# Attention with decaying state and a 16-item feed-forward: another written-out order, fewer VectorE operations for the powers of w, the count for the general path late, the output in 2 KB rows

## The chip, the cores and the metric

The kernel runs on one core of one Trainium2 chip. Its time is the device time of that core in microseconds (us); the profile's span runs from the first to the last instruction of one execution. The engines are called PE (TensorE, matrix products; PEld is its weight load), DVE (VectorE), ACT (ScalarE), POOL (GpSimd) and SP (SyncE, which here issues all transfers).

## What is computed

Four sequences, eight heads, 768 steps, head size 48. A state of 48 x 48 per sequence and head decays by `w` and takes up `k` and `v`; its product with `r` is the attention output. All heads of one step together (384 numbers) then pass a feed-forward of width 2048.

```python
for t in range(S):
    kt, vt, rt = k[:, :, t], v[:, :, t], r[:, :, t]
    cur = np.einsum('bhd,bhe->bhde', u[None] * kt, vt)
    y[:, :, t] = np.einsum('bhd,bhde->bhe', rt, state + cur)
    state = w[None, :, :, None] * state + np.einsum('bhd,bhe->bhde', kt, vt)
...
x = np.ascontiguousarray(attn_out.transpose(0, 2, 1, 3)).reshape(B * S, H * D)
h = x @ w_in
sp = np.maximum(h, 0.0) + np.log1p(np.exp(-np.abs(h)))
g = h * erf(sp)
return (g @ w_out).astype(np.float32)
```

## The kernel before

**Chunks.** The 768 steps are cut into six stretches of 128. One stretch of one sequence is a chunk; there are 24, numbered stretch by stretch, and four chunks of one stretch make a block of 512 tokens (blocks 0 to 5). A chunk arrives in two transfers, r and k by `load_a` (L66) and v with a second copy of k and r by `load_b` (L69). Chunk 3 takes a buffer of x; all others share three, so from chunk 4 on a load waits until an earlier chunk is finished with.

Within a chunk the steps are handled together. k and r are multiplied by powers of w, downwards and upwards: `prep_k` (L189), `prep_r` (L193) and, for the second copy of k, `prep_n` (L197). `a_step` (L238, tile A) makes all products of r and k, PE. The diagonal is u times k times r, summed: `diag_a` (L201), `diag_b` (L204), `diag_c` (L208, tile q), spread to a matrix by `diag_m` (L219 on ACT, L221 elsewhere, tile am); `predicated` (L244, two DVE instructions) lays the lower triangle of A over it. `y_step` (L261) multiplies am with v and, from chunk 4 on, r with the state (tile sbd): 32 products for the first four chunks, 56 for the others. `ds_product` (L280) makes the state's increment, which `s_add` (L292, L294) takes up and `s_mul` (L298) decays. `x_step` puts y into its block's x as a rounded part (L301, ACT) and the rest (L304, DVE).

**Items.** One block times one of 16 slices of the feed-forward's width is an item, 96 in all. `f1` (L327) makes h from x in nine products: three column groups, each as w_in's rounded part with both parts of x, and w_in's rest with x's rounded part. Then come `act_a` (L334), `act_b` (L338), `act_z` (L343, DVE), `act_c` (L347), `act_d` (L351), `act_e` (L355), `act_g` (L359, DVE), `act_h` (L365, the rounded part of g) and `act_l` (L370, the rest of g, on DVE or POOL). `f2` (L386) adds the item to acc in nine products. h has three buffers in PSUM, which the first chunks' tiles use too. Blocks 0 and 1 run interleaved, eight slices of each and then eight of each again, and their first halves' sums go to DRAM and back (tiles part).

**Weights.** w_in and w_out arrive as 64-bit floats in eight pieces each (`fetch_w`, L102). `load_w` makes of each a rounded part and a rest in six steps: a (L118, ACT), b, c, d (L120, L122, L125, all DVE), e (L128, ACT), f (L130, DVE or POOL), 768 numbers on each of 128 partitions. An item waits for its slice.

**Powers of w.** At the start (L150 to L169) DVE squares w seven times (tile wp), takes the reciprocal of each square, and doubles the run of powers pw six times with them; from pw come wr and wk, half of each by ACT. Where a w lies outside 0.7 to 0.97, a general path is needed: `bad` (L162) marks it, a product `cnt` (L419) counts, and DVE reduces the count to `fi` (L421). Every engine reads fi (L487) before the branch to the general path, which these inputs don't take.

**Order.** Nothing is scheduled by a program here. The string `ORDER` (L587 on) lists all steps one by one; each engine gets its instructions in that order and waits only for what an instruction reads or for a buffer to come free. A letter says which step, the number which chunk, piece or item, and a sign which engine: none for DVE, `+` for POOL, `*` for ACT. U, L and F are transfers; K, R, N are the products with powers of w; Q a, b, c and M the diagonal; A, P, Y, D, S, X as above; C the weights' six steps; f, a, b, z, c, d, e, g, h, l, p an item's; O the output; W n are n products on dummy data that keep PE busy (L87).

**Output.** The result stands transposed in DRAM. One block's third of the 384 columns is a tile of 128 x 512, copied from acc (L405 to L408) and stored by `put_out` (L391) as four pieces of 512 bytes on each partition, into rows of 4 x 768.

## Time and profile before

| | |
|---|---|
| three runs | 542.63, 544.76, 546.79 us; median 544.76 |
| profiled execution | 544.89 us, span 543.1 |
| mean granted PE clock | 0.990 |
| busy: PE, DVE, ACT, POOL | 515.7, 365.8, 397.9, 184.0 us |
| DMA packets | 20775, of which 10992 under 2 KB |

The profile's page and the trace behind it are read by view. A group row gives line, engine, operation, what is written and read, shapes and count, then the busy time, the mean of one in ns, and the idle time just before them with what ended it. A stage row gives a stretch and each engine's busy time in it, then PE's granted clock and the DMA engines' share and GB/s. A row of the chain of waits or of the timeline has the start, the length, and the instructions, with their count behind an x. A matmul's end is modelled, so the length of a single one overlaps the next; a row over many back to back is right.

### The profile page before, as it was taken

The page shows a single profiled execution, that of the slowest core. Times are in us where ns is not written, and L with a number is a line of the kernel's source. Part 1 is how long each engine was busy: PE and PEld are TensorE (multiplying, and loading weights), DVE is VectorE, ACT ScalarE, POOL GpSimd, SP SyncE. Part 2 cuts the span into 40 slices and gives each one's busy share as a digit, 9 for nine tenths or more (in the row PEclk, how much of TensorE's full clock was granted, in tenths as well). Part 3 has the DMA queues.
Part 4 walks back from the last instruction along what each step waited for, and adds up shares of the span by engine and source line. Part 5 has one row for each costly group of instructions (what it writes and reads, how often), then busy time and mean ns, then how long its engine had stood idle before and what let it go on. Part 6 is the DMA issues. An engine that isn't in the chain of part 4 may idle for free.

```text
span 543.1 us, 10439 instructions
## 1 busy us (share of the span) xinstructions
PE 515.7 (95%) x4155; PEld 394.0 (73%) x4162; DVE 365.8 (67%) x604; ACT 397.9 (73%) x753; POOL 184.0 (34%) x158
## 2 busy tenths in 40 slices
PE   7778999899999999989999899999999999999994
PEld 3446777677878777767777677788777787878873
DVE  7999999999686567595499568344399435243442
ACT  3346798898999783767567498878588686698873
POOL 3665514550323424641286244100065221111100
PEclk9989999999999999989999999999999999999998
DMA  8664236623430503702222150000350000100002
GB/s 303 253 216 156 66 110 218 252 79 116 162 111 1 158 26 105 247 1 86 64 109 86 40 189 1 1 1 2 108 206 1 1 1 1 50 9 1 1 1 64
DMA packets 20775, 48.91 MB, mean 90 GB/s; under 512 B 1648, under 2 KB 10992, under 8 KB 20720
## 3 DMA queue, kind: packets, MB, share of 16 engines
q1 hardware_dynamic: 20720, 48.18, 25.7%
q8 instruction: 35, 0.57, 0.4%
q14 instruction: 20, 0.16, 0.1%
HBM read 41.88 MB, written 6.29 MB: 89 GB/s over the span
## 4 chain that ended last, share of the span: by engine, by line
PE 60%; DVE 21%; ACT 12%; issue 3%; DMA 1%; POOL 1%; SPq 0%; ACTq 0%; DVEq 0%
PE h L327 26%; PE acc L386 26%; PE y L261 4%; DVE s L343 2%; ACT s L347 2%; DVE gl L370 2%; DVE s L359 2%; PE A L238 2%; DVE att L193 2%; DVE am L244 2%; DVE wt L125 2%; ACT gh L365 2%; ACT s L355 2%; PE dummy L87 2%; ACT s L351 2%
## 5 line engine op out<-in xcount | busy, mean ns | idle before, releaser
L327 PE MATMUL h<-x,wih 128*128 128x512 f32 x576 | 183.9, 400 | 3.0 <-DVE s L359 2.5
L327 PEld LDWEIGHTS h<-x,wih 128*128 128x128 f32 x576 | 106.2, 188 | 32.7 <-DVE s L359 6.4
L370 POOL TENSOR_TENSOR gl<-s,gh 128x512 fp32r<-128x512 f32 x47 | 62.1, 1322 | 171.0 <-ACT gh L365 165.9
L386 PE MATMUL acc<-gl,woh 128*128 128x512 f32 x288 | 115.2, 400 | 5.0 <-DVE gl L370 4.5
L386 PE MATMUL acc<-gh,woh 128*128 128x512 f32 x288 | 116.6, 405 | 0.2 <-ACT gh L365 0.2
L327 PE MATMUL h<-x,wil 128*128 128x512 f32 x288 | 113.9, 396 | 0.7 <-POOL wil L130 0.7
L386 PE MATMUL acc<-gh,wol 128*128 128x512 f32 x288 | 114.2, 396 | 0.0
L359 DVE SCALAR_TENSOR_TENSOR s<-s,h 128x512 f32<-128x512 f32 x96 | 65.5, 684 | 67.2 <-ACT s L355 67.1
L343 DVE SCALAR_TENSOR_TENSOR s<-s,h 128x512 f32<-128x512 f32 x96 | 65.3, 682 | 57.3 <-ACT s L338 37.8
L365 ACT CAST gh<-s 128x512 fp32r<-128x512 f32 x96 | 58.9, 615 | 37.8 <-DVE s L359 21.7
L347 ACT ACTIVATE s<-s 128x512 f32<-128x512 f32 x96 | 60.1, 627 | 29.5 <-DVE s L343 28.9
L334 ACT ACTIVATE s<-h 128x512 f32<-128x512 f32 x96 | 56.3, 587 | 23.9 <-PE h L327 23.6
L386 PEld LDWEIGHTS acc<-gl,woh 128*128 128x128 f32 x288 | 54.6, 190 | 20.2 <-DVE gl L370 6.5
L386 PEld LDWEIGHTS acc<-gh,woh 128*128 128x128 f32 x288 | 54.4, 189 | 15.7 <-issue 2.0
L327 PEld LDWEIGHTS h<-x,wil 128*128 128x128 f32 x288 | 54.2, 188 | 14.2 <-POOL wil L130 1.1
L386 PEld LDWEIGHTS acc<-gh,wol 128*128 128x128 f32 x288 | 54.6, 189 | 12.2
L351 ACT ACTIVATE s<-s 128x512 f32<-128x512 f32 x96 | 60.0, 627 | 1.3
L338 ACT ACTIVATE s<-s 128x512 f32<-128x512 f32 x96 | 60.0, 626 | 1.0
L355 ACT ACTIVATE s<-s 128x512 f32<-128x512 f32 x96 | 59.9, 626 | 1.0
L370 DVE TENSOR_TENSOR gl<-s,gh 128x512 fp32r<-128x512 f32 x49 | 39.7, 811 | 18.5 <-ACT gh L365 17.8
L244 DVE COPY_PREDICATED am<-mask,A 64x256 f32<-64x256 uint32 x96 | 39.1, 442 | 8.7 <-PE A L238 4.4
L219 ACT ACTIVATE am<-ident,q 128x128 f32<-128x128 f32 x96 | 30.2, 390 | 8.5 <-DVE q L208 8.5
(73 smaller groups left out, 537.4 us busy)
## 6 DMA issues: line engine op xcount, KB each, us to landing
att<-in_att_dram SPq DMA_DIRECT2D x24, 608.0 KB, 6.1
att<-in_att_dram SPq DMA_DIRECT2D x24, 512.0 KB, 4.5
raw<-in_win_dram SPq DMA_DIRECT2D x8, 768.0 KB, 4.5
raw<-in_wout_dram SPq DMA_DIRECT2D x8, 768.0 KB, 4.3
out_dram<-o SPq DMA_DIRECT2D x18, 256.0 KB, 2.7
part<-o SPq DMA_DIRECT2D x6, 256.0 KB, 2.1
o<-part SPq DMA_DIRECT2D x6, 256.0 KB, 4.7
ub<-in_u_dram SPq DMA_DIRECT2D x1, 192.0 KB, 2.6
```

The costliest lines, as they stand in the source:

```text
L244: nc.vector.copy_predicated(out=am[r, :, c], data=ap[r, :, c], mask=m[r, hh:hh + 1, c].to_broadcast([r.stop - r.start, NPAIR, H]))
L327: nc.tensor.matmul(out=h, lhsT=w[:, f, q, :], rhs=x[:, xi, q, :], start=k == 0, stop=k == 8)
L334: nc.scalar.activation(out=s1, in_=e["h"], func=AF.Tanh, bias=FB0, scale=FA0)
L338: nc.scalar.activation(out=s1, in_=s1, func=AF.Tanh, bias=FB1, scale=FA1)
L343: nc.vector.scalar_tensor_tensor(out=e["s"], in0=e["s1"], scalar=FG, in1=e["h"], op0=ALU.mult, op1=ALU.add)
L347: nc.scalar.activation(out=s, in_=s, func=AF.Tanh, bias=FB2, scale=FA2)
L351: nc.scalar.activation(out=s, in_=s, func=AF.Square, bias=FB3, scale=FA3)
L355: nc.scalar.activation(out=s, in_=s, func=AF.Square, bias=FB4, scale=FA4)
L359: nc.vector.scalar_tensor_tensor(out=s, in0=s, scalar=FC, in1=ff[n]["h"], op0=ALU.subtract, op1=ALU.mult, reverse0=True)
L365: nc.scalar.copy(out=e["gh"], in_=e["s"])
L370: eng.tensor_tensor(out=e["gl"], in0=e["s"], in1=e["gh"].bitcast(F32), op=ALU.subtract)
L386: nc.tensor.matmul(out=acc[e], lhsT=w[:, f, es], rhs=g, start=first and i == 0, stop=last and i == 2)
```

## The change

The arithmetic stays. What differs:

- The powers of w: the seven squares come first, one reciprocal takes all seven, then come the six doublings. The upper half of wr is made by POOL.
- `bad`, the count and its reduction become `count_bad`, called by a new step Z; in the order it stands at one place, between item 76's steps e and g.
- `f2` can make one third of an item's products; the last three items are written so (p93x, p93y, p93z and so on).
- The output lies in DRAM by blocks, so that a tile of 128 x 512 is stored with 2 KB on each partition. The host's final transposition changes with it.
- ORDER is new throughout. It has the same steps, but 73 in place of 76 dummy products after the first 16, and the choice of DVE, POOL or ACT differs for many steps.
- `turn_k` and `copy_k` are new functions that no step of this order calls.

```diff
     for n in range(7):
+        nc.vector.tensor_tensor(out=wp[:, n + 1, 0], in0=wp[:, n, 0], in1=wp[:, n, 0], op=ALU.mult)
+    nc.vector.reciprocal(out=wp[:, 0:7, 1], in_=wp[:, 0:7, 0])
+    nc.vector.tensor_copy(out=pw[:, 1, :, 0], in_=wp[:, 0, 1])
+    for n in range(6):
         m = 1 << n
-        nc.vector.tensor_tensor(out=wp[:, n + 1, 0], in0=wp[:, n, 0], in1=wp[:, n, 0], op=ALU.mult)
-        nc.vector.reciprocal(out=wp[:, n, 1], in_=wp[:, n, 0])
-        if n == 0:
-            nc.vector.tensor_copy(out=pw[:, 1, :, 0], in_=wp[:, 0, 1])
-        if n < 6:
-            nc.vector.tensor_tensor(out=pw[:, :, :, m:2 * m], in0=pw[:, :, :, 0:m],
-                                    in1=wp[:, n, :, :, None].to_broadcast([PR, 2, NPAIR, m]), op=ALU.mult)
-    bad = const.tile([PR, NPAIR], F32, name="bad")
-    nc.vector.tensor_tensor(out=bad, in0=wp[:, 0, 0], in1=wc, op=ALU.not_equal)
+        nc.vector.tensor_tensor(out=pw[:, :, :, m:2 * m], in0=pw[:, :, :, 0:m],
+                                in1=wp[:, n, :, :, None].to_broadcast([PR, 2, NPAIR, m]), op=ALU.mult)
     nc.scalar.copy(out=wr[:, :, 0:H], in_=pw[:, 0])
-    nc.vector.tensor_tensor(out=wr[:, :, H:C], in0=pw[:, 0], in1=wp[:, 6, 0, :, None].to_broadcast([PR, NPAIR, H]),
+    nc.gpsimd.tensor_tensor(out=wr[:, :, H:C], in0=pw[:, 0], in1=wp[:, 6, 0, :, None].to_broadcast([PR, NPAIR, H]),
                             op=ALU.mult)
...
-    def put_out(n, e, cols=None):
+    def put_out(n, e, blk=None):
+
         b = order[n][0]
-        nc.sync.dma_start(out=outT[e * P:(e + 1) * P, :, cols if cols is not None else slice(b * C, (b + 1) * C)],
-                          in_=outs[n, e].rearrange("p (s c) -> p s c", c=C))
+        o = outT[b] if blk is None else outT[bass.ds(blk, 1)].rearrange("a p n -> (a p) n")
+        nc.sync.dma_start(out=o[e * P:(e + 1) * P], in_=outs[n, e])
...
-    cnt = ps1.tile([1, NPAIR], F32, tag="A0", name="cnt")
-    nc.tensor.matmul(out=cnt, lhsT=mask[:PR, 0, P - 1:P], rhs=bad, start=True, stop=True)
     fi = const.tile([1, 1], I32, name="fi")
-    nc.vector.tensor_reduce(out=fi, in_=cnt, axis=AX.X, op=ALU.max)
+
+    def count_bad():
+
+        bad = const.tile([PR, NPAIR], F32, name="bad")
+        nc.vector.tensor_tensor(out=bad, in0=wp[:, 0, 0], in1=wc, op=ALU.not_equal)
+        cnt = ps1.tile([1, NPAIR], F32, tag="A0", name="cnt")
+        nc.tensor.matmul(out=cnt, lhsT=mask[:PR, 0, P - 1:P], rhs=bad, start=True, stop=True)
+        nc.vector.tensor_reduce(out=fi, in_=cnt, axis=AX.X, op=ALU.max)
+
...
-U0 L0a L1a L0b F00 R0 T0 K1 R1 L2a K0 W3 A1 Q0a A0 L2b Q0b Q0c N0+ C00a F10 M00* W3 D0 C00b K2 M01* S0b R2+ P00 L3a
...
+U0 L0a L0b L1a R0 L2a T0 K0 Q0a+ L2b A0 K1 L1b R1 K2 W4 A1 R2 F00 Q0b Q2a+ Q0c M00* N0 F10 Q2b+ W8 D0 M01* P00 Q1a+
...
+z78 a79 g77 c78 b79 d78 Y22 h77 e78 l77 g78 p76 X22a X22b z79 c79 f80 h78 d79 l78 e79 g79 p77 a80 b80 z80 p78 c80 h79
...
```

How the order moves instructions shows at three places. In these lists att0 is chunk 0's tile, wk and wr the powers of w, wkn wk transposed, ub u for all partitions, wt a weight piece in work; the numbers behind the last underscore tell buffers apart.

First the head of DVE's queue, where the first chunk products wait for the powers of w. Before, from the last doubling on:

```order
L159 TENSOR_TENSOR pw_112<-pw_112,wp_109 112x8x32
L154 TENSOR_TENSOR wp_109<-wp_109 112x4
L155 RECIPROCAL wp_109<-wp_109 112x4
L162 TENSOR_TENSOR bad_136<-wp_109,wc_83 112x4
L164 TENSOR_TENSOR wr_110<-pw_112,wp_109 112x4x64
L168 TENSOR_TENSOR wk_111<-pw_112,wp_109 64x4x64
L168 TENSOR_TENSOR wk_111<-pw_112,wp_109 48x4x64
L421 TENSOR_REDUCE fi_166<-cnt_164 1x1
L193 TENSOR_TENSOR att0_169<-att0_169,wr_110 112x512
L189 TENSOR_TENSOR att1_171<-att1_171,wk_111 112x512
L193 TENSOR_TENSOR att1_171<-att1_171,wr_110 112x512
L189 TENSOR_TENSOR att0_169<-att0_169,wk_111 112x512
```

Now, from the same doubling on:

```order
L158 TENSOR_TENSOR pw_112<-pw_112,wp_109 112x8x32
L165 TENSOR_TENSOR wk_111<-pw_112,wp_109 64x4x64
L165 TENSOR_TENSOR wk_111<-pw_112,wp_109 48x4x64
L190 TENSOR_TENSOR att0_158<-att0_158,wr_110 112x512
L186 TENSOR_TENSOR att0_158<-att0_158,wk_111 112x512
L186 TENSOR_TENSOR att1_161<-att1_161,wk_111 112x512
L190 TENSOR_TENSOR att1_161<-att1_161,wr_110 112x512
L186 TENSOR_TENSOR att2_164<-att2_164,wk_111 112x512
L190 TENSOR_TENSOR att2_164<-att2_164,wr_110 112x512
L214 TENSOR_TENSOR att0_158<-att0_158 128x384
```

The square and reciprocal behind the doubling, `bad`, half of wr and the reduction of the count have left the queue here. The first products are chunk 0's r and k, which follow the powers at once, then k and r of chunks 1 and 2; chunk 0's first u product (L201, now L211) has gone to POOL, the second is L214. In SP's queue chunk 1's first transfer now stands behind both of chunk 0's.

Next DVE's queue between the last part of x for block 0 and the first DVE step of item 0 (tile s2_0), which waits for item 0's products and two steps of ACT. Before:

```order
L304 TENSOR_TENSOR x0_326<-y3_592,x0_326 128x3x128
L294 TENSOR_TENSOR sbd_145<-sbd_145,ds4_611 48x4x48 x2
L298 TENSOR_TENSOR sbd_145<-sbd_145,wp_109 48x4x48
L130 TENSOR_TENSOR wol_92<-wt10_492,woh_91 128x768
L201 TENSOR_TENSOR att6_547<-att6_547,ub_85 128x384
L189 TENSOR_TENSOR att7_622<-att7_622,wk_111 112x512
L120 TENSOR_SCALAR wt01_658<-wt01_658 128x768
L304 TENSOR_TENSOR x1_665<-y4_560,x1_665 128x3x128
L343 SCALAR_TENSOR_TENSOR s2_0_672<-s1_0_662,h0_631 128x512
```

Now:

```order
L314 TENSOR_TENSOR x0_345<-y3_543,x0_345 128x3x128
L218 TENSOR_REDUCE q4_583<-att4_341 128x8
L254 COPY_PREDICATED am4_1_586<-mask_94,A4_1_524 64x4x64
L254 COPY_PREDICATED am4_1_586<-mask_94,A4_1_524 128x4x64
L254 COPY_PREDICATED am4_0_592<-mask_94,A4_0_523 64x4x64
L254 COPY_PREDICATED am4_0_592<-mask_94,A4_0_523 128x4x64
L218 TENSOR_REDUCE q5_616<-att5_476 128x8
L353 SCALAR_TENSOR_TENSOR s2_0_618<-s1_0_610,h0_573 128x512
```

Eight instructions lay between the two, among them a weight's rest (L130) and a k product (L189), which now stand elsewhere; now there are six, of chunks 4 and 5.

Last SP's queue from the last chunk's load to the end. Before:

```order
L69 DMA att23_4310<-in_att_dram 128x1216
L391 DMA out_dram<-o79_0_4964 512x1x128
L391 DMA out_dram<-o79_2_4978 512x1x128
L391 DMA out_dram<-o79_1_4998 512x1x128
L391 DMA out_dram<-o95_0_5471 512x1x128
L391 DMA out_dram<-o95_1_5474 512x1x128
```

Now:

```order
L69 DMA att23_4343<-in_att_dram 128x1216
L512 TENSOR_LOAD fi_156
L403 DMA out_dram<-o79_0_4977 128x512
L403 DMA out_dram<-o79_1_4981 128x512
L403 DMA out_dram<-o79_2_5011 128x512
L403 DMA out_dram<-o95_0_5462 128x512
L403 DMA out_dram<-o95_1_5468 128x512
```

SP's read of fi (TENSOR_LOAD) stood behind the first loads of chunks 0 to 3 and now stands behind chunk 23's, ahead of block 4's output; the count it waits for is made between the acc products of items 73 and 74. The stores have become 128 rows of 512 numbers in place of 512 of 128.

More of the change, by code (lines that the diff above doesn't have):

```diff
@@ L197, in prep_n, with turn_k, copy_k @@
         eng.tensor_tensor(out=t, in0=t, in1=wknf, op=ALU.mult)
+    def turn_k(g):
+        tp = (ps3 if g < 4 else ps1).tile([P, NPAIR, PR], F32, tag="h" if g < 4 else "A1", name=f"kt{g}")
+        for p in range(NPAIR):
+            nc.tensor.transpose(out=tp[:, p, :], in_=chunks[g][:PR, 512 + p * C:512 + (p + 1) * C],
+                                identity=ident[:PR, 0, :PR])
+        st_.setdefault(g, {})["kt"] = tp
+    def copy_k(g):
+        o = chunks[g][:, K0:R0].rearrange("p (a b d) -> p a b d", b=2, d=D)
+        for hh in range(2):
+            nc.scalar.copy(out=o[:, :, hh], in_=st_[g]["kt"][:, :, 64 * hh:64 * hh + D])
     def diag_a(t, eng):
@@ L373, in body, with f2 @@
     part = {}
-    def f2(n):
+    def f2(n, part_e=None):
         b, f = order[n]
@@ L378, in f2 @@
         last = n + 1 == len(order) or order[n + 1][0] != b
-        if first:
+        if first and part_e in (None, 0):
             for e in range(NQ):
                 acc[e] = ps1.tile([P, TB], F32, tag=f"acc{e}", name=f"acc{n}_{e}")
-        d = ff.pop(n)
-        for e in range(NQ):
+        d = ff[n]
+        for e in range(NQ) if part_e is None else (part_e,):
             es = slice(e * P, (e + 1) * P)
@@ L433, in body @@
             act_l(num, eng)
+        elif what == "p" and sub in "xyz":
+            f2(num, "xyz".index(sub))
         elif what in steps:
             steps[what](num)
+        elif what == "N" and eng is nc.scalar:
+            copy_k(num)
         elif what in preps:
@@ L443, in body @@
             across(wk)
+        elif what == "V":
+            turn_k(num)
+        elif what == "Z":
+            count_bad()
         elif what == "Q":
@@ new lines @@
+b26 S9c O231b z26 O231c f27 X10a S9b L12b c26 S9d X10b d26 R12 e26 f28 a27 g26 b27 K12 z27 Q12a+ f29 c27 a28 Q12b d27
+Q12c N12+ b28 A12 e27 M120+ a29 g27 M121* p24 P120 b29 P121 p25 h26 l26 z28 Y12 c28 h27 d28 l27+ D12 X12a e28 f30 X12b
+g28 S12b S12a S12d+ z29 f31 a30 S12c c29 b30 d29 D10 a31 p26 S10b L13a e29 S10d b31 g29 S10a L13b S10c p27 h28 L14a
+l28 R13+ z30 L14b p28 c30 K13+ h29 d30 L15a e30 l29 A13 R14 L15b z31 K14+ p29 g30 c31 h30 Q13a d31 Q13b f32 l30 O311a
+e31 N13 O312a Q13c R15+ g31 M130* p30 M131+ a32 P130 h31 K15 b32 f33 P131 l31+ z32 Q15a c32 p31 Q15b a33 d32 Q15c N15+
@@ new lines @@
+b33 O311b e32 z33 Y13 O311c O312b c33 g32 O312c d33 D13 Q14a X13a f34 e33 S13a L16a S13b S13c+ h32 X13b S13d+ g33
+O310a l32 h33 L16b f35 Q14b a34 l33+ Q14c b34 M140* z34 K16+ O310b f36 a35 O310c M150* R16+ p32 c34 Q16a a36 Q16b d34
+N14 b35 M141 e34 A15 z35 N16+ b36 g34 c35 p33 M151+ P150 h34 d35 P151 e35 l34 f37 g35 z36 h35 Q16c c36 l35+ f38 a37
+d36 b37 e36 z37 p34 a38 g36 c37 b38 d37 f39 h36 e37 l36+ g37 p35 a39 z38 b39 c38 d38 f40 h37 e38 l37 g38 Y15 a40 z39
+b40 c39 D15 X15a d39 f41 S15b S15d e39 X15b g39 S15a f42 S15c a41 b41 A14 p36 P140 P141 p37 h38 l38 z40 Y14 a42 c40
@@ L650 @@
+c87 d87 e87 f88 g87 h87 l87+ f89 a88 b88 z88 f90 c88 a89 d88 b89 p87 e88 z89 a90 g88 c89 h88 f91 b90 l88 d89 z90 e89
+c90 g89 p88 a91 d90 b91 h89 f92 e90 l89+ g90 h90 z91 p89 a92 l90+ c91 b92 d91 z92 f93 e91 c92 g91 d92 h91 f94 a93 l91+
+e92 b93 g92 p90 z93 a94 b94 c93 d93 p91 h92 e93 l92+ g93 f95 h93 z94 l93 c94 d94 p92 a95 e94 b95 g94 z95 p93x h94 p93y
+c95 l94 d95 p93z e95 p94x g95 p94y h95 p94z l95 p95x p95y O950a p95z O950b O951a O951b O952a O952b
 """
@@ L708 @@
     B, S = inputs["r"].shape[0], inputs["r"].shape[2]
-    out = nc.dram_tensor("out_dram", (384, B, S), F32, kind="ExternalOutput").ap()
+    out = nc.dram_tensor("out_dram", (S // C, 384, B * C), F32, kind="ExternalOutput").ap()
     with tile.TileContext(nc, schedule_with_timeline_sim=True) as tc:
@@ L712 @@
     res = run_bass_kernel_spmd(nc, [feed], core_ids=[0])
-    return np.ascontiguousarray(np.asarray(res.results[0]["out_dram"]).reshape(384, -1).T)
+    y = np.asarray(res.results[0]["out_dram"]).reshape(S // C, 384, B, C)
+    return np.ascontiguousarray(y.transpose(2, 0, 3, 1)).reshape(B * S, 384)
```

109 lines of the change are left out of this document (47 added, 62 removed).

## The prediction

> **What bounds the kernel now.** I read the page's head first, then the groups, then the busy time by stage, then the chain of waits.
>
> ```profile
> span 543.1 us, 10439 instructions
> PE 515.7 (95%) x4155; PEld 394.0 (73%) x4162; DVE 365.8 (67%) x604; ACT 397.9 (73%) x753; POOL 184.0 (34%) x158
> ```
>
> PE is the engine to look at, but its 95% holds warm-up products and overlapping ends, so I count what its work costs back to back.
>
> ```profile
> L327 PE MATMUL h<-x,wih 128*128 128x512 f32 x576 | 183.9, 400 | 3.0 <-DVE s L359 2.5 <-DVE x L304 0.5
> L386 PE MATMUL acc<-gl,woh 128*128 128x512 f32 x288 | 115.2, 400 | 5.0 <-DVE gl L370 4.5 <-POOL gl L370 0.4
> 176.90 6.27 PE h L327 x27
> 382.73 1.67 PE y L261 x56
> 386.69 1.02 PE A L238 x24
> 13.31 0.56 PE L280 MATMUL ds<-att 128*48 128x48 f32 x16
> ```
>
> An item has nine products to h (576 of the rows' products are six for each of 96 items) and nine to acc (288 are three); 27 take 6.27 us, so nine take 2.09, and 96 items take 192 x 2.09 = 401.3 us. A y costs 1.67 (56 products) or, for the first four chunks with 32 products, 0.96: 37.2 for 24. Score products (A) cost 1.02 x 24 = 24.5, state products (ds) about 0.5 x 20 = 10. Together **473.0 us** of work that neither version can drop. The other 70.1 us are lag: PE waiting, warming, or done. Where they arise shows in the start of items (first row item 0, then 2 and 16), the last products, and the stages.
>
> ```profile
> 44.09 0.58 PE L327 MATMUL h<-x,wih 128*128 128x512 f32 x1
> 58.22 0.50 PE L327 MATMUL h<-x,wih 128*128 128x512 f32 x1
> 132.67 0.39 PE L327 MATMUL h<-x,wih 128*128 128x512 f32 x1
> 533.93 2.14 PE acc L386 x8
> 0.00:58.20 58.20, 47.01 (x621) 27.40 (x628) 52.43 (x110) 26.84 (x62) 34.19 (x36) 0.97 0.62 224
> 58.20:132.70 74.50, 71.22 (x606) 54.12 (x605) 72.28 (x111) 64.34 (x122) 26.16 (x19) 1.00 0.40 139
> 310.00:536.00 226.00, 224.75 (x1512) 177.60 (x1510) 113.87 (x184) 175.22 (x324) 53.40 (x44) 1.00 0.11 37
> ```
>
> (The columns behind the length are the busy time of PE, weight load, DVE, ACT, POOL.) In the old order 20.0 us of real PE work stand ahead of item 2 and 87.5 ahead of item 16 (16 h and 13 acc groups, 10 A, 9 ds, 9 y). So the lag is 38.2 us at item 2 and 45.2 at item 16; another 17.9 arise up to the end of the last product at 536.1, and 7.0 lie behind it. In the first 132.7 us DVE is busy for 124.7: **the fill is bound by DVE**, everything behind it by PE, with DVE half loaded at the end.
>
> **The start.** The old DVE queue reaches its first chunk product here:
>
> ```profile
> 6.36 0.84 DVE L168 TENSOR_TENSOR wk<-pw,wp 64x256 f32<-64x256 f32 x2
> 8.32 0.15 DVE L421 TENSOR_REDUCE fi<-cnt 1x1 int32<-1x4 f32 x1 [1.12 <-PE cnt L419]
> 8.50 0.69 DVE L193 TENSOR_TENSOR att<-att,wr 112x512 f32<-112x512 f32 x1
> ```
>
> It waits 1.12 us for the count, which sits in PE's queue behind 16 warm-up products. The change takes count and reduction out; six small reciprocals and one half of wr go too. The squares now form a chain of seven dependent steps instead of lying between other work, which gives back some of it, and wr's second half on POOL must end before the first product. I put that product at 7.3: **-1.2 us** (bounds: 0, if the chain or POOL ends as late as the count did; -1.3, if it follows 6.36 + 0.84 at once). The count itself now stands between item 73's and item 74's acc products; DVE's reduction waits there for at most those nine, 2.1 us, and queued behind it is an activation step whose acc products are 8 us of PE work away. That slack hides it: 0; without it 2.1 us.
>
> **The fill.** Up to item 16 the two orders ask PE for exactly the same work, 87.5 us. DVE has 192 instructions ahead of it before and 193 now. Taking the shortest of each kind, five more r products and two more k products (0.69 each, above), one n product, three state products and steps b, c and d of one more weight piece, set against six u products, two am, one weight's rest, one step g and three items' rests: **+0.5 us**. POOL has 41 before and 36 now. That matters because some DVE kinds are stretched in this stage and some are not:
>
> ```profile
> L125 DVE SCALAR_TENSOR_TENSOR wt<-raw,wt 128x768 int32<-128x768 int32 x11 | 13.7, 1242 | 0.0
> L122 DVE SCALAR_TENSOR_TENSOR wt<-raw,wt 128x768 int32<-128x768 int32 x11 | 10.7, 977 | 0.1
> L370 DVE TENSOR_TENSOR gl<-s,gh 128x512 fp32r<-128x512 f32 x12 | 10.3, 865 | 0.0
> L343 DVE SCALAR_TENSOR_TENSOR s<-s,h 128x512 f32<-128x512 f32 x15 | 10.0, 675 | 0.0
> L120 DVE TENSOR_SCALAR wt<-wt 128x768 int32<-128x768 int32 x11 | 10.0, 906 | 0.0
> L197 DVE TENSOR_TENSOR att<-att,wkn 128x384 f32<-128x384 f32 x6 | 6.3, 1054 | 0.0
> 235.91 0.55 DVE L201 TENSOR_TENSOR att<-att,ub 128x384 f32<-128x384 f32 x1
> L338 ACT ACTIVATE s<-s 128x512 f32<-128x512 f32 x96 | 60.0, 626 | 1.0
> ```
>
> L343, which reads h, stays at 0.675 whatever POOL does. L197 has the size of L201, which takes 0.55 alone, and averages 1.054. Summed: 11 x 0.29 (L125), 11 x 0.36 (L120), 12 x 0.18 (L370), 6 x 0.5 (L197), and 2.3 for the other chunk products make 14.5 us of stretch over 41 POOL instructions, 0.35 us each. Five fewer: **-1.8 us** (0 to -4: the ones that go may have met no stretchable work, or each cost 0.8).
>
> Against it, the front of the new DVE queue has less to fill gaps with. It takes k and r of chunks 0, 1, 2 in a row, so the third product stands behind chunk 1's load, now third in SP's queue; and between the last piece of x for block 0 and the first step of item 0 lie only six DVE instructions, under 3 us, against the 3.3 us that item 0's products (2.09) and two activations (0.63 each, last row) take. Three such gaps of nearly 0.6 us: **+1.7 us** (0 to +4). The new order reaches item 2 with 75 DVE instructions and 41.6 us instead of 83 and 46.2, at 18.8 instead of 20.0 us of PE work; I expect it near 53.5, but between items 2 and 13 it then asks DVE for 64.0 us beside 56.1 of PE work, so most of that lead is spent again. Fill with start: -1.2 + 0.5 - 1.8 + 1.7 = **-0.8 us**, item 16 at 131.9.
>
> **Behind the fill.** Of the 17.9 us, about 7 are handovers of 0.1 to 0.2 us (nine products behind a y take 2.29 instead of 2.09, first row), of which a few dozen stay in any order. The other 11 sit in a dozen places, most of it before an acc product that waits for g's rest (second row); the largest, 4.0 us near 233, shows how one arises:
>
> ```profile
> 415.79 2.29 PE h L327 x9
> PE acc L386 <- DVE gl L370: 3.6, 3, 2.3
> 231.31 4.07 DVE L193 TENSOR_TENSOR att<-att,wr 112x512 f32<-112x512 f32 x1
> 235.31 0.68 DVE L370 TENSOR_TENSOR gl<-s,gh 128x512 fp32r<-128x512 f32 x1
> 231.38 1.27 POOL L189 TENSOR_TENSOR att<-att,wk 112x512 f32<-112x512 f32 x1
> 232.61 1.27 POOL L370 TENSOR_TENSOR gl<-s,gh 128x512 fp32r<-128x512 f32 x1
> ```
>
> One r product needs 4.07 us instead of 0.69 while POOL runs instruction on instruction, and the residual that PE needs stands behind it. That happens where attention work crowds. Cut into pieces of 20 us of PE work, the old order's heaviest pieces behind the fill hold 19.4 us of DVE work with 13.4 of POOL (220 to 240) and 18.3 with 11.5 (340 to 360). The new order's hold 19.0 with 1.3 (100 to 120), 16.5 with 11.1 and 16.5 with 8.6, though one has 14.0 with 14.7 of POOL (340 to 360). Totals are the same. I take a third of the 11 us off: **-3.5 us** (bounds: -9, if only small waits remain; +5, if the POOL-heavy piece makes a wait like the one above and a bit more).
>
> The Trainium skill ("SBUF — State Buffer", section Who interferes with whom) says that a DVE instruction with two SBUF inputs and a reading GpSimd instruction exclude each other for a whole instruction. By that alone a wait would end with the POOL instruction in flight, 1.3 us at most; the 4.07 us row went through several, so the measurement decides, and a run of POOL instructions is the dangerous thing.
>
> **The end.** Splitting the last items' acc groups by output third moves no product. Behind the last product the outputs follow:
>
> ```profile
> 536.55 0.37 ACT L406 COPY o<-acc 128x256 f32<-128x256 f32 x1 [0.33 <-DVE o L405]
> L391 SPq DMA_DIRECT2D out_dram<-o x18: 533/542/651, 176.3 to 536.9; - x18
> DMA to landing us min/median/max: 2.6/2.7/4.8
> part<-o SPq DMA_DIRECT2D x6, 256.0 KB, 2.1
> GB/s 0 0 0 0 0 0 0 0 63 289 292 281 289 178 246 281 300 281 271 25 0 0 0 0 0 0 0 66 300 284 289 295 164 0 0 0 0 0 0 0
> GB/s 0 0 0 0 0 0 0 0 229 393 377 393 377 295 33 0 0 0 0 0 0 0 0 0 0 360 360 410 344 442 181 0 0 0 0 0 0 0 0 0
> ```
>
> The last output, issued at 536.9, takes the longest 4.8 us to land; the program ends 1.4 us later. The first GB/s row is three outputs in 512 B pieces (469.5 to 477), at 280 to 300; the second is two stores of partial sums, the same 256 KB in 2 KB rows, at 360 to 400, which land in 2.1 us. The new outputs are such stores. Last landing 2.4 us behind its issue: **-2.4 us** (bounds: 0, and 4.8 - 2.1 = -2.7). The Trainium skill ("DMA: Bandwidth & Descriptors", Specifications) puts line rate from 512 B on; by that the term would be 0 and the time 540.6. The two rows above disagree.
>
> **Sum.** -0.8 - 3.5 - 2.4 = -6.7: last product at 531.8, span 536.4. The profiled execution took 544.89 us by its own clock, 1.8 more than its span, and the median is 544.76, so the two stand alike: **538.2 us**.
>
> **Rivals.** *The order gains nothing (541.7).* The waits behind the fill are as many, elsewhere, and the new gaps eat the rest: -0.8 and -2.4 remain. For it: same totals on DVE and POOL, and the fill's end fixed by 193 instructions against 192. Against: the flatter pieces. *Rows of 2 KB don't help (540.6).* The 4.8 us would be a late straggler of any last store; for it: other outputs of 512 B landed in 2.6. *The lead at item 2 survives (532).* PE is 3.5 us less late there; if the work that the new order puts between items 2 and 13 is not needed at once, that lead stays, and with two thirds of the 11 us gone: -1.2 - 2.3 - 7 - 2.4 = -12.9. *Slower: locks in the fill (550.7).* Up to item 0 POOL still has 13 chunk instructions (14 before), now beside a DVE queue that holds seven more r and k products up to item 16, the kind that took 4.07 us. DVE binds there, so stretch lands in full. At 0.35 us for each of 36 POOL instructions it is 12.7 us; at 0.7 it is 25, so that +10.7 stands in place of the -1.8 and the sum is +5.8: 550.7. It decides from 0.54 on, where it eats the 6.7.
>
> **Chances.** Forecast 0.42; nothing from the order 0.20; rows don't help 0.10; lead survives 0.18; locks 0.10. A measurement of this kernel can tell about 1%, 5.4 us: faster means below 539.3. The forecast (give or take 4 us) lies below that in two of three cases, the lead in all, the other two in one of four: 0.53 faster, 0.37 within 1%, 0.10 slower. The bounds together reach from 528 to 554; 530.5 to 546.5 leaves out the best combination and the locks.
>
> **What would show it.** The first chunk product near 7.3 us; item 0 near 40, item 2 near 53.5, item 16 near 132; DVE still busy without break up to there, its chunk products below 1 us on average; no wait of 4 us on PE behind 140; outputs landing in 2.0 to 2.4 us; about 6900 fewer DMA packets. Item 16 later than 135, or a DVE product of 3 us in the fill, would make the forecast wrong on the slow side; item 16 before 129 on the fast side.

## The result and the profile after

The changed kernel takes **530.66 us** (median of 4 runs, 529.08 to 531.08) where the kernel before, on the same chip, takes 544.27: ratio 0.974, 95% interval 0.970 to 0.978. The forecast was 538.2. The direction was right, and the measured time lies just inside the stated range of 530.5 to 546.5; the size, 6.6 us forecast and 13.6 measured, was not. The profiled execution took 529.08 us with a span of 527.3.

First the page's head:

```profile
span 527.3 us, 10438 instructions
PE 508.5 (96%) x4159; PEld 393.8 (75%) x4159; DVE 348.7 (66%) x602; ACT 396.9 (75%) x757; POOL 170.6 (32%) x153
```

Then, from the timeline, the first chunk product, the starts of items 0, 2 and 16, and the last product:

```profile
7.54 0.69 DVE L190 TENSOR_TENSOR att<-att,wr 112x512 f32<-112x512 f32 x1
37.72 0.59 PE L337 MATMUL h<-x,wih 128*128 128x512 f32 x1
52.36 0.73 PE L337 MATMUL h<-x,wih 128*128 128x512 f32 x2
128.15 0.63 PE L337 MATMUL h<-x,wih 128*128 128x512 f32 x2
521.70 0.40 PE L396 MATMUL acc<-gh,wol 128*128 128x512 f32 x1
```

PE's useful work is the same 473.0 us, so the difference is lag alone: what the work costs back to back is taken off, and what is left is PE waiting, warming up or done. Item 16 starts at 128.15 instead of 132.67: its lag (start less 87.5) falls from 45.2 to 40.7, by **4.5**. From there to the end of the last product (522.09) another 8.4 us arise instead of 17.9: **9.5** less. Behind the last product lie 5.2 us instead of 7.0: **1.8** less. Together 15.8, the difference of the two spans. The spans differ by more than the medians: the profiled execution after was the shortest of its four.

In the fill, DVE shows where the time came from. Before, up to item 16, then after:

```profile
0.00:132.70 132.70, 118.23 (x1225) 81.52 (x1233) 124.72 (x220) 91.18 (x183) 60.35 (x55) 0.99 0.50 176
```

```profile
0.00:128.15 128.15, 115.51 (x1226) 81.22 (x1227) 115.69 (x212) 95.99 (x203) 51.67 (x51) 1.00 0.54 188
```

DVE is busy for 9.0 us less and idle for 4.5 us more (12.5 instead of 8.0), which makes the 4.5. The work is nearly the same (eight instructions fewer, small ones of the start); most instructions are shorter. The groups that the prediction quoted as stretched, after, and behind them one that went the other way:

```profile
L125 DVE SCALAR_TENSOR_TENSOR wt<-raw,wt 128x768 int32<-128x768 int32 x12 | 12.4, 1037 | 0.3
L120 DVE TENSOR_SCALAR wt<-wt 128x768 int32<-128x768 int32 x12 | 7.4, 617 | 0.0
L380 DVE TENSOR_TENSOR gl<-s,gh 128x512 fp32r<-128x512 f32 x9 | 6.2, 683 | 0.0
L194 DVE TENSOR_TENSOR att<-att,wkn 128x384 f32<-128x384 f32 x7 | 4.2, 599 | 0.0
L190 DVE TENSOR_TENSOR att<-att,wr 112x512 f32<-112x512 f32 x9 | 7.8, 866 | 0.1
```

The means were 1.242, 0.906, 0.865 and 1.054; they are 1.037, 0.617, 0.683 and 0.599. The r products (last row) average 0.866, where four of them averaged 0.683 before.

Behind item 16, PE's waits (sum, times, longest), before and then after:

```profile
PE acc L386 <- DVE gl L370: 3.6, 3, 2.3
PE h L327 <- DVE s L359: 1.3, 3, 0.6
PE acc L386 <- POOL gl L370: 0.4, 2, 0.2
...
```

```profile
PE h L337 <- DVE s L369: 0.6, 1, 0.6
PE acc L396 <- DVE gl L380: 0.2, 1, 0.2
```

Next to nothing is left of the waits that the profile shows. The outputs, from the page and from the view of their tile:

```profile
DMA packets 13863, 48.91 MB, mean 93 GB/s; under 512 B 1648, under 2 KB 1776, under 8 KB 13808
out_dram<-o SPq DMA_DIRECT2D x18, 256.0 KB, 2.2
```

6912 packets fewer, and a median landing of 2.2 us instead of 2.7.

### The profile page after: what moved, and what is told of

Same layout as the page of the kernel before. It is cut to its first block, busy times and chain, and to the rows that moved or that the text cites. A ratio compares the mean times of both kernels' runs of the same rounds, so it can differ in the third digit from the quotient of the medians.

```text
span 527.3 us, 10438 instructions
## 1 busy us (share of the span) xinstructions
PE 508.5 (96%) x4159; PEld 393.8 (75%) x4159; DVE 348.7 (66%) x602; ACT 396.9 (75%) x757; POOL 170.6 (32%) x153
## 4 chain that ended last, share of the span: by engine, by line
PE 71%; DVE 17%; ACT 7%; issue 2%; DMA 1%; POOL 0%; SPq 0%; DVEq 0%; ACTq 0%; POOLq 0%
PE acc L396 32%; PE h L337 31%; PE y L271 5%; PE A L248 3%; DVE wt L125 2%; DVE am L254 2%; DVE wt L122 2%; ACT am L229 2%; DMA att<-in_att_dram 1%; DVE s L353 1%; DVE att L190 1%; DVE s L369 1%; DVE wt L120 1%; PE ds L290 1%; DVE q L218 1%
## 5 line engine op out<-in xcount | busy, mean ns | idle before, releaser
L380 POOL TENSOR_TENSOR gl<-s,gh 128x512 fp32r<-128x512 f32 x48 | 64.3, 1339 | 223.8 <-ACT gh L375 197.7
L396 PE MATMUL acc<-gl,woh 128*128 128x512 f32 x288 | 114.0, 396 | 0.2 <-DVE gl L380 0.2
L344 ACT ACTIVATE s<-h 128x512 f32<-128x512 f32 x96 | 56.7, 590 | 26.3 <-PE h L337 22.2
L337 PEld LDWEIGHTS h<-x,wil 128*128 128x128 f32 x288 | 54.3, 189 | 12.9 <-DVE wil L130 0.4
L396 PEld LDWEIGHTS acc<-gl,woh 128*128 128x128 f32 x288 | 54.4, 189 | 12.5 <-DVE gl L380 0.7
L380 DVE TENSOR_TENSOR gl<-s,gh 128x512 fp32r<-128x512 f32 x48 | 36.1, 753 | 17.7 <-ACT gh L375 17.6
L229 ACT ACTIVATE am<-ident,q 128x128 f32<-128x128 f32 x100 | 31.3, 389 | 9.6 <-DVE q L218 9.5
```

The costliest lines, as they stand in the source:

```text
L337: nc.tensor.matmul(out=h, lhsT=w[:, f, q, :], rhs=x[:, xi, q, :], start=k == 0, stop=k == 8)
L344: nc.scalar.activation(out=s1, in_=e["h"], func=AF.Tanh, bias=FB0, scale=FA0)
L380: eng.tensor_tensor(out=e["gl"], in0=e["s"], in1=e["gh"].bitcast(F32), op=ALU.subtract)
L396: nc.tensor.matmul(out=acc[e], lhsT=w[:, f, es], rhs=g, start=first and i == 0, stop=last and i == 2)
```

## The experiments

One table for all, beside the two kernels. The ratio is to the kernel before, run beside it on the same chip (its medians were 544.1 to 545.6). "Lag behind" is the end of the last product less 473.0 less item 16's lag. "Stretch" is, over DVE's instructions, the duration less the shortest of its kind and shape in the same execution, counted where it is over 0.05 us and summed ahead of item 16 and behind it; the expectations below count the smaller differences too (17.9 and 28.7 for the kernel before). The last three columns are of one profiled execution each.

| kernel | median us | ratio, interval | item 16 | lag behind | stretch |
|---|---|---|---|---|---|
| before | 544.27 | | 132.7 | 17.9 | 15.6 / 22.2 |
| changed | 530.66 | 0.974 (0.970 to 0.978) | 128.2 | 8.4 | 4.7 / 10.4 |
| rows_only | 543.12 | 0.997 (0.994 to 0.999) | 133.8 | 17.1 | 17.1 / 22.9 |
| start_only | 543.15 | 0.999 (0.997 to 1.001) | 130.8 | 17.8 | 14.9 / 22.6 |
| order_only | 532.29 | 0.977 (0.974 to 0.981) | 128.8 | 8.4 | 5.0 / 10.3 |
| fill_new | 542.25 | 0.997 (0.994 to 0.999) | 129.4 | 18.0 | 4.9 / 23.1 |
| steady_new | 541.80 | 0.996 (0.994 to 0.997) | 133.5 | 14.4 | 16.2 / 11.2 |
| before_sign | 557.65 | 1.024 (1.019 to 1.030) | 141.5 | 25.5 | 12.1 / 15.5 |
| before_thin | 546.93 | 1.004 (1.000 to 1.007) | 130.0 | 23.3 | 0.6 / 0.1 |
| after_thin | 554.02 | 1.018 (1.014 to 1.022) | 136.1 | 26.9 | 0.5 / 0.4 |
| before_thin2 | 526.53 | 0.965 (0.963 to 0.968) | 123.5 | 8.8 | 0.0 / 0.0 |
| after_thin2 | 526.47 | 0.965 (0.962 to 0.968) | 125.3 | 8.7 | 0.0 / 0.3 |
| before_r14 | 543.99 | 0.999 (0.997 to 1.001) | 133.0 | 16.3 | 16.1 / 22.9 |
| before_thin_l | 539.06 | 0.990 (0.987 to 0.992) | 131.0 | 10.8 | 13.5 / 12.9 |
| before_thin_att | 526.61 | 0.966 (0.963 to 0.968) | 123.3 | 9.7 | 0.2 / 7.0 |
| after_thin_att | 527.70 | 0.967 (0.965 to 0.969) | 127.5 | 8.7 | 1.9 / 3.3 |
| after_k7 | 531.52 | 0.975 (0.972 to 0.977) | 129.7 | 8.7 | 5.6 / 10.0 |
| after_d4l1 | 528.76 | 0.969 (0.966 to 0.972) | 127.8 | 8.7 | 4.7 / 10.3 |

### Which part of the change

**rows_only** is the old kernel with the new `put_out` and the output by blocks; nothing else is touched.

> The old kernel with nothing changed but the output, by blocks in 2 KB rows. Theory (what lies behind the last product shrank from 7.0 to 5.2 us between the two profiles because of the rows): 1.8 us less, ratio 0.9965. Rival (the 4.8 us of the last landing was a straggler that any store can have): no change, ratio 1.000. PE's work up to the last product is the same in both theories, last product at about 536.

**start_only** is the old order with the new powers of w, half of wr on POOL, and the count as step Z:

```diff
-... X23b ...
+... X23b Z0 ...
```

> The old order with the new powers of w, wr's upper half on POOL, and the count behind chunk 23's x. Theory (DVE binds in the fill, so an earlier first chunk product moves everything up to item 16): first product 1.0 us earlier, at 7.5, and 1.0 us less in all, ratio 0.998. Rival (the next wait, for a load or for am, takes it back): first product earlier, time unchanged, ratio 1.000.

**order_only** is the new ORDER (less Z0) with the old powers, count and rows.

> The new order with everything else as before: the old powers of w and early count, and output rows of 512 bytes. If the parts stand beside each other, the order alone gives what is left when the rows' 1.8 us and the start's 1.2 us are taken from the 13.6 us that the whole change gains: 533.6, last product at about 523.5, a tail behind it of about 7. Rival: the fill of the new order needs the earlier start, since its DVE queue has the chunk products first; then item 16 comes later than 130.5 and the whole takes 536 or more.

The order alone makes 12.1 of the 13.6 us. The rows are worth 0.3%, with an interval (0.1 to 0.6%) that leaves out zero. The tails behind the last product agree: over all kernels of this document, 5.1 to 5.8 us in nine profiles with 2 KB rows (mean 5.4) and 6.2 to 7.0 in eleven with 512 B pieces (mean 6.5). By these the rows take off about 1.1 us, and the 1.8 between the first two profiles counts from the longest tail of all. The start is not told from nothing: its first chunk product comes a microsecond sooner, and the interval holds 1. The rival in order_only's expectation, that the new fill needs the earlier start, is out: item 16 comes at 128.8 with the old one.

**fill_new** takes the new order up to step c21 and then every step not yet done in the old order; **steady_new** takes the old order up to C16f and then the rest in the new one. Both keep the old start and rows.

> Old start, old output rows, the new order up to item 21's step c and the old order from there on. Theory (the two parts of the order each carry their own gain; the fill's is the shorter DVE stretch, 7.4 instead of 17.9 us): 3.5 us less than before, ratio 0.9935, with the old waits near 233 and 306 still there. Rival (the gain belongs to how the whole order fits together): the fill's lead is lost again in the old waits, ratio 1.000.

> Old start, old output rows, the old order up to a piece of w_out near item 20 and the new order from there on. Theory (the new order's gain behind the fill is its own): item 16 as late as before, near 132.7, then 9 us less, ratio 0.983; no wait of over 1 us on PE behind 160. Rival (the waits follow from how late the fill is): ratio between 0.993 and 1.000.

Each half carries its own stretch with it: fill_new has the new fill (4.9 ahead) and the old rest (23.1), steady_new the reverse (16.2 and 11.2). fill_new keeps all of the old lag behind item 16 (18.0) and gains 2.0 us, where 3.5 were expected. steady_new should then have had 8.4 but has 14.4, because of the seam: five of the six steps of weight piece 17, which the new order does ahead of the cut and the old one behind it, now all stand at the cut, ahead of chunk 9's part of x, and PE waits for that. The wait, and then the stages of 4 us there:

```profile
PE y L274 <- DVE x L317: 4.2, 1, 4.2
```

```profile
164.00:168.00 4.00, 1.20 (x6) 0.62 (x4) 3.03 (x4) 1.72 (x3) 0.00 (x0) 0.97 0.00 0
168.00:172.00 4.00, 2.64 (x52) 2.67 (x56) 3.23 (x7) 3.89 (x9) 1.18 (x1) 0.50 0.00 0
```

PE works 1.2 of 4 us, and then at half its clock (0.50, the third figure from the end). So steady_new's time says little on the new rest; its stretch does. The two halves' times, 2.0 and 2.4 us, do not add up to the order's 12.1, and how the gain divides between them is not shown by times.

### Engines or places

**before_sign** leaves every step of the old order where it is and gives it the engine of the new order, for 139 steps, as in `l33` to `l33+` or `l34+` to `l34`.

> The old order with every step where it was, but each on the engine that the new order gives it (139 steps change between DVE, POOL and ACT). If the gain lies in which steps run on POOL, the time falls to 537 or less. If it lies in where the steps stand (so that the same engine choice meets other neighbours), the time is 542 or more, and the larger waits behind item 16 are as many, at other places.

It is 2.4% slower than before, although the stretch is smaller: up to item 16, at 141.5, DVE idles for 20.1 us instead of 8.0, longest in sum for ACT's step of the diagonal (4.0 us). So less stretch alone does not make a faster order, and the choice of engines alone does not make the gain. The reverse, the new places with the old engines, was not run; that the gain needs both together is likely and not shown.

### Is it POOL's reading?

**before_thin** and **after_thin** keep order and engines, but a step on POOL reads one column and then writes zeros three times, so that these kernels leave out the products of POOL's steps:

```diff
+class Thin:
+    def tensor_tensor(self, out, in0, in1, op):
+        cut = (slice(None),) * (len(out.shape) - 1) + (slice(0, 1),)
+        self.eng.tensor_tensor(out=out[cut], in0=in0[cut], in1=in1[cut], op=op)
+        for _ in range(3):
+            self.eng.memset(out.bitcast(F32), 0.0)
...
-        eng = {"+": nc.gpsimd, "*": nc.scalar}.get(x[-1], nc.vector)
+        eng = {"+": Thin(nc.gpsimd), "*": nc.scalar}.get(x[-1], nc.vector)
```

> The kernel before, in which every order step given to POOL reads one column of its inputs and then writes zeros over its output three times, so that POOL is as long at it but reads next to nothing: the products of these steps are left out. Theory of collisions: DVE's stretch (17.9 us ahead of item 16, 28.7 behind) comes from instructions that read beside POOL's, and it is this that made the larger waits behind the fill. Then the stretch falls below 3 us in all, item 16 starts 8 to 15 us earlier (about 122), the 4.0 us wait near 233 is gone, the waits of PE over 0.3 us behind item 16 fall from about 10 us to under 2, and the time is about 525. Rival, distances: the waits come from residuals that stand too close before the products that need them, and the stretch only adds to it. Then the fill gains the same, but more than 6 us of waits stay behind it, and the time is 531 or more.

> The changed kernel with the same thinned POOL steps (their products are left out). Theory of collisions: the two orders differ by how often POOL reads beside a DVE product, so without POOL's reads they differ by little: 522 to 526, within 4 us of the kernel before with thinned steps once the output's 1.8 us is set aside. Rival, distances: the new order is better for where it puts the steps, and it stays 8 us or more ahead of the old one also without POOL's reads.

Both expectations missed, for a reason outside both theories. The stretch did go, to 0.7 and 0.9 us in all, but POOL's steps became over a third longer (249.0 us in all instead of 182.2 in the old order). In before_thin the residual's groups are these (writing, then reading):

```profile
L48 POOL MEMSET gl<- 128x512 f32 x141 | 74.8, 531 | 8.2
L46 POOL TENSOR_TENSOR gl<-s,gh 128x1 fp32r<-128x1 f32 x47 | 10.4, 220 | 133.1 <-ACT gh L376 133.0
```

and PE's largest wait behind item 16 is now for POOL:

```profile
PE acc L397 <- POOL gl L48: 5.0, 6, 1.2
```

3 x 0.53 + 0.22 = 1.81 us for a residual that took 1.32. With two writings it is 1.28: **before_thin2** and **after_thin2** differ from the pair above in `range(2)` alone.

> As the thinned kernel before, but with two writings of zeros instead of three, so that a POOL step lasts about as long as the product it replaces (1.3 us for a residual; with three it lasted 1.8 and the waits named POOL). The POOL steps' products are left out. Theory of collisions: without POOL's reads the stretch of DVE is gone, item 16 starts at about 120 and PE's waits over 0.3 us behind it fall from about 10 us to under 3: 524 to 529. Rival, distances: the stretch goes and the fill gains up to 10 us, but the waits behind item 16 stay above 6 us because the order places residuals too close: 531 to 538.

> The changed kernel with the POOL steps thinned in the same way (their products left out). Theory of collisions: it differs from the old order without POOL's reads by 4 us or less beyond the output's 1 us, since both are free of stretch. Rival, distances: it stays 8 us or more ahead. If the order is fitted to the durations that the steps have with POOL's reads, taking these away gains little here: 527 to 531.

**526.53 and 526.47.** POOL's steps are now as long as the ones that they replace (179.5 us in all instead of 182.2 in the old order, 170.2 instead of 168.1 in the new), and without its reads the two kernels take the same time, with 8.8 and 8.7 us of lag behind item 16. The new one has its 2 KB rows in that time: its last product ends at 519.5, the old order's at 517.7, so the new order by itself has no lead left. The theory of distances asked for one of 8 us or more; it falls. All that the new kernel gains beyond its rows lies in how POOL's reading instructions meet DVE's. The old order loses 17.6 us to them, the new kernel 4.2 by the medians and about 5 by the ratios. The thinned steps lack POOL's arithmetic as well as its reads, and these kernels alone do not tell the two apart.

**before_r14** moves one step of the old order:

```diff
-h34 R14 l33 Q14a
+h34 l33 R14 Q14a
```

> The old order with one step moved: chunk 14's r product, the one that took 4.07 us on DVE, stands behind item 33's residual instead of ahead of it. If the residual's place behind the stretched product is what PE waited for, the 4.0 us wait near 233 goes, nothing else moves, and the time falls by 3 to 4 us (540.5 to 541.5). Rival: what PE gains there it loses at the next wait (items 40, 46, 47), and the time stays within 1 us.

The edit did not do what was expected of it, and shows more for that. The timeline of DVE in this kernel:

```profile
230.48 4.12 DVE L370 TENSOR_TENSOR gl<-s,gh 128x512 fp32r<-128x512 f32 x1
234.52 0.68 DVE L193 TENSOR_TENSOR att<-att,wr 112x512 f32<-112x512 f32 x1
```

and that of POOL:

```profile
229.59 1.02 POOL L201 TENSOR_TENSOR att<-att,ub 128x384 f32<-128x384 f32 x1
230.58 1.29 POOL L189 TENSOR_TENSOR att<-att,wk 112x512 f32<-112x512 f32 x1
231.83 1.26 POOL L370 TENSOR_TENSOR gl<-s,gh 128x512 fp32r<-128x512 f32 x1
233.07 0.98 POOL L204 TENSOR_TENSOR att<-att 128x384 f32<-128x384 f32 x1
```

Now the residual itself takes 4.12 us and the r product its 0.68. At this place the hold belongs to the moment, not to the instruction: in both kernels, the DVE product that stands here while POOL runs instruction on instruction stays until the run is over (now 233.07 + 0.98 = 234.05; in the kernel before, 233.84 + 0.98 = 234.82) and ends 0.55 us later. The next one, L193 at 234.52, is at full speed. The time did not move (0.999).

That is not so at every place. Of the 17 DVE instructions of before that are held for over 0.9 us, 13 end behind the one POOL instruction that ran when they began, and for four of these the next POOL instruction followed without a gap. One is another r product; its row, then POOL's:

```profile
293.75 1.68 DVE L193 TENSOR_TENSOR att<-att,wr 112x512 f32<-112x512 f32 x1
```

```profile
293.41 1.47 POOL L189 TENSOR_TENSOR att<-att,wk 112x512 f32<-112x512 f32 x1
294.85 2.07 POOL L201 TENSOR_TENSOR att<-att,ub 128x384 f32<-128x384 f32 x1
```

Here DVE's product ends 0.55 us behind the first of the two, so it got in when POOL passed from one instruction to the next, and POOL's u product is the longer one, 2.07 us where the u product in the run above took 1.02. Which of the two gets in at such a passage is open.

### Which of POOL's steps

**before_thin_l** thins only the residuals on POOL, **before_thin_att** and **after_thin_att** only the attention steps (two writings each). The edit of the last two; in before_thin_l the condition is `x[0] == "l"`:

```diff
-        eng = {"+": Thin(nc.gpsimd), ...
+        eng = {"+": Thin(nc.gpsimd) if x[0] in "KRNQMS" else nc.gpsimd, ...
```

> The old order in which only the residuals on POOL (47 steps l, 44 of them behind item 16) are thinned; the 98 attention and 5 weight steps on POOL still read (the residuals' products are left out). If residuals and attention steps of POOL hold DVE alike, about a third of the 17.6 us that the old order gained without any of POOL's reads comes back, nearly all of it behind item 16: 538, item 16 at 131 to 133. If the runs of attention steps are what holds DVE (a lone residual delays it by 1.3 us at most, a run by 4), the time is 542 or more.

> The old order in which only POOL's attention steps are thinned (powers of w, u products, diagonal, state; their products are left out), while residuals and weight steps still read. If runs of attention steps are what holds DVE: 527 to 531, item 16 near 125, the wait of 4 us near 233 gone. If residuals count alike: about 533 to 535, with PE waits of 0.5 us and more left behind item 16.

> The changed kernel with only POOL's attention steps thinned (their products left out). Without any of POOL's reads it stands at 526.5. If the new order has already placed these steps where they hold nothing up, it gains 3 us or less (527.5 to 530.7) and stays within 3 us of the old order thinned alike. Rival: the old order thinned alike stays 5 us or more behind, because the residuals too are better placed in the new one.

With the attention steps thinned, the old order is at 526.61, as fast as with all thinned; item 16 starts at 123.3, and PE's waits behind it are

```profile
PE h L338 <- DVE s L370: 0.6, 1, 0.6
PE acc L397 <- DVE gl L381: 0.2, 1, 0.2
PE acc L397 <- POOL gl L381: 0.2, 1, 0.2
```

The residuals alone give about 6 us (ratio 0.990), nearly all of it behind item 16 (lag behind 10.8), and nothing that the attention steps have not given already: the two do not add. In the run of POOL instructions above, one of four is a residual, and taking either kind out of such runs would break them; that this is why the two do not add is a reading, not a measurement. 7.0 us of stretch are left behind item 16 in before_thin_att, and only 1.0 us of waits with them: stretch by POOL's residuals and weight steps costs PE next to nothing there. The new order gains only 3 us (4 by the ratios) from the same thinning.

### Two tries at a better order

**after_k7** moves chunk 7's k product on POOL forward, and **after_d4l1** chunk 4's state steps (which change places with chunk 6's), chunk 7's first load and chunk 1's:

```diff
-R7 C12d f7 Q7a ... Q7b+ z6 c5 L8b K7+ Q7c
+R7 K7+ C12d f7 Q7a ... Q7b+ z6 c5 L8b Q7c
```

```diff
-U0 L0a L0b L1a R0
+U0 L0a L1a L0b R0
...
-z3 D6 g2 ... S6a p2 S6b ... D4 a5 f6 d4 S4a L7a l3 C12a S4c S6c L7b
+z3 D4 L7a g2 ... S4a p2 S4b ... D6 a5 f6 d4 S6a l3 C12a S6c S4c L7b
```

> The changed kernel with one step moved: chunk 7's k product on POOL stands right behind its r product on DVE instead of behind the second u product. POOL idles 11.7 us ahead of it, and its chunk's load has landed at 77.5, so chunk 7's scores need not wait 2.4 us near 83. If that wait is lost time, item 16 comes 2 to 3 us earlier and the time is 528 or less. Rival: DVE's queue binds there (it waits 1.4 us in all between 68 and 91), the wait moves to the next item and less than 1 us is gained; or the k product now holds up the DVE product beside it.

> The changed kernel with two edits of its order: chunk 4's state product comes ahead of chunk 6's instead of last, so that chunk 7's first load finds its buffer earlier, and chunk 1's first load stands ahead of chunk 0's second. If chunk 7's late load makes the waits of items 4 and 8 and of chunk 7 (5 us together between 79 and 90) and chunk 1's load the gap of 1.8 us on DVE near 9, item 16 comes 3 to 5 us earlier and the time is 526 to 528. Rival: DVE's work binds the fill all the same (118 of the 128 us ahead of item 16), the waits move to a later place, and the gain is under 1.5 us.

after_k7 gains nothing (531.5): the k product now runs beside chunk 7's r product, which takes 1.78 us where it took 0.69, and item 16 comes no sooner (129.7). DVE's row, then POOL's:

```profile
75.89 1.78 DVE L190 TENSOR_TENSOR att<-att,wr 112x512 f32<-112x512 f32 x1
```

```profile
75.46 1.66 POOL L186 TENSOR_TENSOR att<-att,wk 112x512 f32<-112x512 f32 x1 [9.08 <-DMA att<-in_att_dram]
```

In after_d4l1 the load that was issued at 70.94 goes out at 63.06:

```profile
63.06 0.33 SPq L66 DMA_DIRECT2D att<-in_att_dram  x1
```

and PE's waits from 76 to 92 are what they were:

```profile
PE ds L290 <- DVE am L254: 1.4, 1, 1.4
PE A L248 <- POOL att L186: 0.7, 1, 0.7
```

So these waits did not hang on the load. POOL waits there for DVE (11.7 us for the u product ahead of it), which points to DVE's queue. The median of after_d4l1 was still 1.9 us lower than the changed kernel's, which had been measured at another time, so the two were run side by side:

> The changed kernel itself, beside the two moved order steps of the next run on the same chip. If its 530.7 holds, it is 530 to 531.5; its profiled execution had a span of 527.3, and the executions behind the median were up to 2 us longer.

> The changed kernel with chunk 4's state product, chunk 7's first load and chunk 1's first load earlier, which was 528.8 in another sharing of the chip while its trace had the same span as the changed kernel's (527.2 against 527.3) and the same waits. If the edits do nothing, as the trace says, the two kernels of this pair are within 0.8 us of each other; if the 1.9 us between the medians are theirs, this one is 1.5 us or more below.

531.82 (ratio 0.976, 0.973 to 0.979) and 530.20 (0.974, 0.971 to 0.976). The intervals overlap; over both measurements the ten times of each are 529.1 to 533.0 and 528.5 to 531.4. The pair meets the letter of the second expectation (1.5 us or more below) but does not separate the two kernels. A gain of 0.3% is possible and stays open.

## Why the prediction was wrong

**What held.** PE's useful work, the order's equal demands up to item 16, the fill bound by DVE (though it idles for 12.5 us there, not 8.0), the packets (6912 against "about 6900"), the count at no cost worth naming (PE starts the acc product behind it 0.4 us late, at 437.8), and the direction of the rows: forecast -2.4, measured -1.8 by the first two tails and by rows_only's ratio (0.4 to 3.2 us), and about -1.1 by the tails of all profiles, so the term was too large. The rival that rows do not help is out. The first chunk product came at 7.54 (forecast 7.3).

**The fill: forecast -0.8, measured -4.5.** The step that failed is the price of stretch by the piece: 14.5 us over 41 POOL instructions, 0.35 each, five fewer, -1.8. With five fewer POOL instructions the stretch did not fall by an eighth but from 15.6 to 4.7 us. What counts is not how many POOL instructions a stage has but which DVE instruction runs beside which, and that the order sets. The gaps were larger than put down (DVE idle 4.5 us more, against 1.7) and ate half. Item 0 came at 37.7, not 40, and the lead, which I had expected to be mostly spent by item 13, lived on to item 16: at 128.15 it came ahead of the 129 that the prediction had named as its own sign of being wrong. How much of it lives varies: in after_again item 16 started at 130.8, for the reason told at the end.

**Behind the fill: forecast -3.5, measured -9.5.** This is the larger miss. The prediction had the place (residuals behind a held DVE product), the example (the 4.07 us row) and nearly the bound (-9, if only small waits remain); what remained is what it called handovers, "about 7", and measures 8.4 to 9.1 in the new order. The step that failed reads "Totals are the same. I take a third of the 11 us off." The totals are nearly the same (POOL has 144 such steps before and 138 now), and they do not tell the orders apart: before_thin2 and after_thin2 show that both fit these totals equally well without POOL's reads, and that what separates them is how POOL's and DVE's instructions meet. A share of a third had no row behind it. The flatter pieces quoted there pointed the right way, and the slow rival that followed from counting (locks in the fill) pointed the wrong way: the new fill had more r and k products on DVE and a third of the stretch.

**The rivals.** "The lead survives" was nearest, at 532 and 0.18: it has the lead and two thirds of the waits gone. It took the fill's gain partly from the start, which gave nothing that can be told from zero, instead of from shorter DVE instructions, and so came near the time by a mechanism that is only half the one found.

**One row misread.** The 4.0 us near 233 was taken as one wait. It is 2.3 us of waiting and then slow products. The timeline of PE before, and the stage:

```profile
236.04 0.79 PE L386 MATMUL acc<-gl,woh 128*128 128x512 f32 x1 [2.30 <-DVE gl L370]
...
239.30 0.62 PE L327 MATMUL h<-x,wih 128*128 128x512 f32 x2
```

```profile
230.00:240.00 10.00, 7.70 (x54) 5.75 (x55) 8.29 (x9) 5.49 (x11) 4.83 (x5) 0.83 0.01 2
```

Eight products take 3.26 us (236.04 to 239.30) where eight ninths of 2.09 are 1.86. The granted clock stood in the row of this stage, 0.83, and I read it only as a mean over the whole span, 0.99.

The Trainium skill ("SBUF — State Buffer", Who interferes with whom) says that a DVE instruction with two SBUF inputs contends with a GpSimd instruction that reads SBUF and not with one that only writes. The thinned kernels agree: two writings in place of the reads leave none of 37.8 us of stretch in before_thin2, and 0.3 of 15.1 in after_thin2. That the hold ends with the one instruction in flight is borne out by 13 of the 17 holds counted above and not by the costliest; in before_r14 it lasted through three that began after it.

## What to carry to other kernels

Where two engines hold each other up, count neither their busy time nor their instructions; list, for each held instruction, what ran on the other engine at that moment, and who waits behind it. A cheap experiment prices the whole of it before an order is judged: let one engine write without reading, for the same time (check its length), and see what the kernel takes. Moving the one instruction that was seen to be held moved the hold to its neighbour here; what took the long hold away was to thin the run of instructions on the other engine.

## What the chip showed that I had not expected

A wait of PE can cost half as much again as its length, because a lower granted clock can follow it: the 2.30 us wait above is followed by 1.4 us lost on slow products. It does not always follow. The changed kernel was profiled twice, and in stages of 2 us from 82 to 92 (88 to 90 left out), a first execution (span 527.3) reads

```profile
82.00:84.00 2.00, 0.75 (x18) 0.51 (x20) 1.53 (x4) 1.85 (x5) 2.00 (x3) 1.00 1.04 427
84.00:86.00 2.00, 0.76 (x27) 0.52 (x19) 1.01 (x3) 2.00 (x7) 1.83 (x2) 1.00 0.97 399
86.00:88.00 2.00, 1.86 (x68) 1.84 (x72) 2.00 (x5) 1.94 (x4) 0.35 (x1) 1.00 0.05 16
90.00:92.00 2.00, 2.00 (x10) 1.63 (x9) 1.99 (x4) 1.75 (x6) 1.92 (x3) 1.00 0.97 368
```

and the second (after_again, span 530.6)

```profile
82.00:84.00 2.00, 1.42 (x32) 1.03 (x32) 0.83 (x3) 2.00 (x7) 2.00 (x3) 1.00 1.01 412
84.00:86.00 2.00, 0.62 (x15) 0.59 (x16) 1.71 (x5) 1.97 (x5) 1.14 (x1) 0.65 0.68 282
86.00:88.00 2.00, 2.00 (x45) 1.78 (x44) 1.97 (x5) 1.60 (x3) 1.04 (x1) 0.50 0.03 8
90.00:92.00 2.00, 1.93 (x4) 1.43 (x5) 1.95 (x5) 0.78 (x3) 0.53 (x2) 0.50 0.65 199
```

The same program with the same waits keeps its clock once and loses half of it for about 10 us the other time, although PE was busier ahead of the loss (2.0 of the first 4 us) than where the clock stayed (1.5); why it fell only once is not shown. Item 7 starts 0.7 us earlier in the second execution, item 10 2.5 us later and item 16 2.6 us later (130.8 instead of 128.2), so the loss falls where the clock is low. The old order has such dips at 30 to 40 and at 230 to 240. The ten executions of the changed kernel fit this with one exception: the four with a mean granted clock of 0.991 or less took 531.1 to 533.0 us, the six above it 529.1 to 531.3, the longest of them at 0.999. Such a dip makes a spread of some 2 us between executions of one kernel, as large as what the last experiments looked for.
